# Infini-attention beside a gated MLP: gate logits on VectorE, finer buffers and pieces, and a new instruction order

## The chip, the cores and the metric

The kernel runs on one core of a Trainium2 chip. The metric is the device time of one execution in microseconds (us). A core has TensorE (PE, matmuls into PSUM), VectorE (DVE), ScalarE (ACT, activation functions), GpSimd (POOL) and SyncE (SP, which issues most DMAs). The engines run side by side; each one works through its own queue in order and waits there on semaphores.

## The reference, cut to what matters

A token's output is a mix of two branches, and the mixing weight comes from the token's gate logit `z = sum(x * gate_w)`:

```python
g = sigmoid((x * gate_w).sum(-1, keepdims=True))      # x: 2048 tokens x 512
return g * A(x) + (1 - g) * B(x)

def A(x):      # 32 heads of 16, 4 segments of 512 tokens
    q, k, v = x @ wq, x @ wk, x @ wv
    for s in range(4):
        p = softmax(q_s @ k_s.T * 0.25 + causal_mask)
        a_dot = p @ v_s
        a_mem = (phi(q_s) @ M) / (phi(q_s) @ z + 1e-6)
        o_s = sigmoid(beta) * a_mem + (1 - sigmoid(beta)) * a_dot
        M, z = M + phi(k_s).T @ v_s, z + phi(k_s).sum()
    return concat(o) @ wo
    # phi(t) = t + 1 where t > 0, else exp(t)

def B(x):      # 1792 hidden columns
    return (gelu_tanh(x @ w_gate) * (x @ w_up)) @ w_down
```

## The kernel before

All work is cut into named tasks. A list written out in the source, `ORDER` (lines 32 to 135), says in which order they are emitted, and so in which order each engine meets its own. `@A`, `@D`, `@P` behind a name choose ScalarE, VectorE or GpSimd; letters behind `#` name the buffers that the task takes. `Sched.run` (line 168) only checks that dependencies come earlier in the list. A task's number is segment and chunk, or, for logit slots, 0 to 79.

Tasks on TensorE. `mm4` (line 350) does a 128-column product as four 32-column tiles that run side by side, a round; before the first logit slot it is one matmul on the whole array (line 354), later four (line 358).

- `warm`, `xt`, `fill`, `k0f`: the start. x of segment 0 is transposed on TensorE, copied to `xT` (`ext`, in two token halves), and `k0f<fc>.<half>` makes the first k.
- `q`, `k`, `v`, `up`: groups of four rounds of 512 columns into one of two PSUM banks `gen` (a, b). `eq`, `ek`, `ev`, `eup` empty them; `ko` makes the copy of k for odd heads.
- `gt<s>.<pair>`: a pair of gate groups into a two-bank tile `lg` (three of them, a to c); `egt` is its gelu on ScalarE.
- `lg<n>`: a slot of logits for part of eight heads, twenty slots a segment (five for each chunk c of eight heads), in row tiling, into two `lg` tiles. `ex<n>a`, `ex<n>b` are the exps on ScalarE (line 662) into one of twelve `pT` buffers, `as<n>a/b` the causal masks on GpSimd (line 671).
- `pv<s>.<c>e/o`: probabilities times v for even and odd heads; it needs the masks of three slots. `epv`, `r`, `rg`, `n`, `m`, `o` on VectorE (and `m` on GpSimd) normalize, add the memory part and transpose back into `xT`.
- `M`, `den`, `num`: memory update and readout; `rma`, `rmr`, `rmg`, `nm` scale it. `E`, `Q`, `Em`, `ph`: phi; `pk`: its transpose by DMA, issued on SP.
- `dn<s>.<qt>.<hs>` (14 rounds) and `wo<s>.<qt>.<c>` (4 rounds) add up an output tile of 128 tokens in one bank; `os` scales it into one of four `osb` buffers, `st` stores it.
- `gz` (line 506): the gate logits of all tokens as 16 matmuls with `gate_w` repeated in 32 columns (`gwB`); `egz` transposes them, `zsp` (32 small GpSimd copies, lines 523 and 524) spreads them into `G2` and `omz`, `g2` and `omz` make the mixing weights. `bps` spreads beta with a small matmul, `tb` is its tanh.

`G`, the gated hidden values, has one buffer of 14 x 512 columns per segment, three in turn. In slots 1 and 4 of a chunk the logits come in pieces of 2, 1 and 1 blocks of 128 columns (line 630), and `pv` reads them as 2, 1 and 1. The last output tile is one bank, read in two halves:

```python
halves = [(0, D // 2), (D // 2, D)] if split else [(0, D)]
...
for n, (lo, hi) in zip(("DVE", "ACT"), halves):
```

Of the kernel before, what the change touches and what calls it, by code (L numbers as in the profile page):

```python
# [8 lines left out]
AF = mybir.ActivationFunctionType  # L9
# [23 lines left out]
in.x3 in.x2 in.x1 in.wo in.wup in.be in.gw in.wga in.wv in.wg0 in.wq in.wk in.wka in.xb in.xn  # L33
warm#a warm.free open#babca xt0.0 xt1.0 xt2.0 xt3.0 fill ext0.0 ext1.0 ext2.0 k0f0.0 k0f1.0 xt0.1
xt1.1 xt2.1 ext0.1 xt3.1 ext1.1 ext2.1 ext3.0 k0f0.1 ext3.1 k0f1.1 k0f2.0 k0f3.0 k0f2.1 k0f3.1
q0.2#a ek0.0@A ek0.1@D q0.3#b ko0.0@P Ek0.0 gt0.0#b eq0.3@D eq0.2@D ek0.3@A Qk0.0 gt0.1#c ek0.2@D
egt0.0 Emk0.0 ko0.1@D phk0.0 q0.0#b v0.2#a egt0.1 gt0.5#a Ek0.1 gt0.3#b egt0.5 gt1.4#c eq0.0@A
gt1.0#a ev0.2@A egt0.3 gt1.2#b egt1.0 egt1.4 gt0.4#a egt1.2 gt1.5#c egt0.4 pk0.0 gt0.6#b gt1.1#a
egt0.6 wdn egt1.5 gt1.3#b egt1.1 gt0.2#c egt1.3 bps#b gt1.6#a egt0.2 ebps v0.0#a egt1.6 lg0#bc
ev0.0@D v0.1#b ex0a#a q0.1#a ev0.1@D omg v0.3#b eq0.1@D ex0b#b as0a lg1#ab ev0.3@D up0.0#a ex1a#c  # L40
as0b up0.1#b eup0.0 ex1b#d Emk0.1 lg2#ca eup0.1 up0.2#a ex2a#e as1b gwB up0.3#b eup0.2 ex2b#f
Qk0.1 lg3#bc eup0.3 up0.4#a ex3a#g as2b as2a up0.5#b eup0.4 ex3b#h as1a lg4#ab eup0.5 up0.6#a
ex4a#i up0.7#b eup0.6 ex4b#j as4a lg5#ca eup0.7 pv0.0e#a as4b ex5a#k ko0.2@D up0.8#b phk0.1
epv0.0e ex5b#l lg6#bc eup0.8 up0.9#a ex6a#a up0.10#b eup0.9 as3b pk0.1 ex6b#b as3a lg7#ab ko0.3@P
eup0.10 pv0.0o#a ex7a#c up0.11#b epv0.0o ex7b#d as6b lg8#ca eup0.11 up0.12#a as6a ex8a#e as7b
up0.13#b eup0.12 as5b ex8b#f as7a lg9#bc eup0.13 gz#a as8a ex9a#g as8b as5a up1.0#b egz ex9b#h
as9a lg10#ab zsp eup1.0 pv0.1e#a ex10a#i up1.2#b epv0.1e ex10b#j lg11#ca eup1.2 up1.1#a ex11a#a
k1.0#b eup1.1 ex11b#b lg12#bc ek1.0@D k1.1#a ex12a#k r0.0 q1.0#b ek1.1@A as9b g2 up1.3#a eq1.0@A
as11b ex12b#l pv0.1o#b eup1.3 lg13#ab Ek1.0 rg0.0 epv0.1o as12b up1.4#a as12a ex13a#c up1.5#b
as10a eup1.4 as11a ex13b#d lg14#ca eup1.5 as10b up1.6#a Emk1.0 ex14a#e n0.0 q1.1#b eup1.6 ex14b#f  # L50
# [12 lines left out]
lg25#ab eup2.3 as20b q2.1#b ex25a#i o0.2 pv1.0e#a nm1.1@D eq2.1@A as25a lg26#ca epv1.0e ex25b#j
num1.2#b as24b enum1.2 up2.4#a as24a ex26a#a nm1.2@P dn0.0.0#b eup2.4 dn0.0.1 ex26b#b dn0.0.2
lg27#bc o0.1 as25b dn0.0.3 dn0.0.4 as26a ex27a#k rg0.3 num1.3#a dn0.0.5 as26b dn0.0.6 enum1.3
dn0.0.7 dn0.0.8 ex27b#l as27a lg28#ab n0.3 pv1.0o#a Ek2.0 as27b dn0.0.9 epv1.0o dn0.0.10 dn0.0.11
dn0.0.12 ex28a#c Emk2.0 dn0.0.13 wo0.0.0 o0.3 pv1.1e#a ex28b#d Qk2.0 as28a wo0.0.1 lg29#ca epv1.1e
wo0.0.2 ex29a#e ko1.2@D wo0.0.3 as28b up2.5#a os0.0@D ex29b#f ko1.3@D lg30#bc st0.0 r1.0 up2.6#b
pk1.1 eup2.5 ex30a#g as29b v2.0#a eup2.6 as29a ex30b#h rg1.0 lg31#ab ev2.0@D pv1.1o#b ex31a#a
dn0.1.0#a epv1.1o dn0.1.1 dn0.1.2 dn0.1.3 ex31b#b n1.0 lg32#ca phk2.0 dn0.1.4 v2.2#b ex32a#i  # L70
dn0.1.5 ev2.2@D dn0.1.6 ex32b#j lg33#bc dn0.1.7 v2.3#b as31a ex33a#c as32b dn0.1.8 ev2.3@D dn0.1.9
ex33b#d as30b lg34#ab as32a dn0.1.10 dn0.1.11 ex34a#e as31b dn0.1.12 dn0.1.13 wo0.1.0 m1.0@P
up2.7#b ex34b#f lg35#ca as34a eup2.7 wo0.1.1 ex35a#k wo0.1.2 as34b wo0.1.3 up2.8#b as33b os0.1@A
as30a lg36#bc as33a eup2.8 v2.1#a r1.1 nm1.3@D k2.2#b ev2.1@A Eq2.0 dn0.2.0#a ek2.2@D dn0.2.1
# [976 lines left out]
```

## Time and profile before

| | |
|---|---|
| time, median of 3 runs | 275.52 us (275.51 to 275.94) |
| profiled execution: span, first to last instruction | 274.6 us (274.58); its own time is not given apart |
| mean granted TensorE clock | 0.997 |
| TensorE / ScalarE / VectorE / GpSimd busy | 97 / 81 / 59 / 57% |
| ScalarE table loads | 13, 1.283 us each |
| exps | 160, 153.9 us busy |
| HBM read / written | 8.13 / 2.10 MB |
| SP's x2 and x3 transposes | issued from 16.86 to 29.0 us |
| `wup` issued, landed | 14.36 us, 8.5 us later |

A busy PE includes time in which matmuls are pipelined, so a share of 97% doesn't say that no time is lost; the distance from one start to the next does. Tables are loaded on ScalarE when it changes between exp and gelu.

### The profile page before, as it was taken

The page shows a single profiled execution, that of the slowest core. Times are in us where ns is not written, and L with a number is a line of the kernel's source. Part 1 is how long each engine was busy: PE and PEld are TensorE (multiplying, and loading weights), DVE is VectorE, ACT ScalarE, POOL GpSimd, SP SyncE. Part 2 cuts the span into 40 slices and gives each one's busy share as a digit, 9 for nine tenths or more (in the row PEclk, how much of TensorE's full clock was granted, in tenths as well). Part 3 has the DMA queues.
Part 4 walks back from the last instruction along what each step waited for, and adds up shares of the span by engine and source line. Part 5 has one row for each costly group of instructions (what it writes and reads, how often), then busy time and mean ns, then how long its engine had stood idle before and what let it go on. Part 6 is the DMA issues. An engine that isn't in the chain of part 4 may idle for free.

```text
span 274.6 us, 10880 instructions
## 1 busy us (share of the span) xinstructions
PE 267.1 (97%) x4877; PEld 132.2 (48%) x4877; DVE 162.7 (59%) x309; ACT 222.6 (81%) x242; POOL 156.5 (57%) x285
## 2 busy tenths in 40 slices
PE   8999999999999999999999999999999999899994
PEld 7644444444445554444455564444454454354551
DVE  1420017765889568887366757767558768376361
ACT  2598569989999968999877888989999997869411
POOL 8230003798634966864915847675467667887600
PEclk9999999999999999999999999999999999999998
DMA  7998780020002000002004200000000001001002
GB/s 228 363 252 191 165 258 2 2 42 4 4 2 41 5 2 0 2 5 60 2 2 80 43 24 0 2 2 21 2 5 21 2 2 41 21 5 41 21 5 78
DMA packets 22231, 14.07 MB, mean 51 GB/s; under 512 B 14120, under 2 KB 21160, under 8 KB 22184
## 3 DMA queue, kind: packets, MB, share of 16 engines
q1 hardware_dynamic: 21208, 12.52, 17.9%
q8 instruction: 38, 0.62, 1.0%
q10 hardware_dynamic: 976, 0.85, 0.9%
q14 instruction: 9, 0.07, 0.1%
HBM read 8.13 MB, written 2.10 MB: 37 GB/s over the span
## 4 chain that ended last, share of the span: by engine, by line
PE 86%; DVE 5%; POOL 4%; DMA 2%; issue 1%; ACT 0%; SPq 0%; POOLq 0%; DVEq 0%
PE dn L358 20%; PE up L358 17%; PE gt L354 9%; PE lg L639 8%; PE gt L358 8%; PE pv L690 6%; PE v L358 4%; PE k L358 4%; PE q L358 4%; POOL rm L869 3%; PE k L354 2%; DMA wk<-in_A_wk_dram 1%; DVE G L562 1%; PE q L354 1%; DMA out_dram<-osb 1%
## 5 line engine op out<-in xcount | busy, mean ns | idle before, releaser
L662 ACT ACTIVATE pT<-lg 128x1024 bf16<-128x1024 f32 x160 | 153.9, 1025 | 14.0 <-PE lg L639 11.4
L671 POOL TENSOR_SCALAR_AFFINE_SELECT pT<-pT 128x512 bf16<-128x512 bf16 (+1 forms) x160 | 86.7, 571 | 63.9 <-ACT pT L662 63.5
L358 PE MATMUL dn<-wdn,G 128*32 128x512 bf16 x896 | 61.4, 380 | 0.9 <-DVE Tm L896 0.9
L358 PE MATMUL up<-xT,wup 128*32 128x512 bf16 x896 | 56.3, 380 | 0.4 <-DVE T L708 0.2
L562 DVE TENSOR_TENSOR G<-up,G 128x512 bf16<-128x512 f32 x56 | 38.5, 688 | 26.4 <-PE up L358 25.0
L553 ACT ACTIVATE G<-gt 128x1024 bf16<-128x1024 f32 x28 | 27.8, 1023 | 11.6 <-PE gt L354 6.4
L358 PEld LDWEIGHTS <-wup 128*32 128x32 bf16 x896 | 23.1, 96 | 22.8 <-issue 4.5
L358 PEld LDWEIGHTS <-G 128*32 128x32 bf16 x896 | 22.7, 96 | 20.6 <-issue 4.1
L708 DVE STREAM_TRANSPOSE T<-pv 128x512 f32<-128x512 f32 x32 | 22.8, 713 | 14.2 <-PE pv L690 13.9
L216 DVE CAST vz<-v 128x512 bf16<-128x512 f32 x13 | 9.0, 689 | 30.2 <-PE v L354 24.2
L358 PE MATMUL gt<-xT,wga 128*32 128x512 bf16 x448 | 26.4, 379 | 0.0
L354 PE MATMUL gt<-xT,wga 128*128 128x512 bf16 x112 | 24.7, 379 | 0.0
L690 PE MATMUL pv<-pT,vz 128*32 128x256 bf16 (+2 forms) x640 | 23.4, 273 | 0.2 <-DVE osb L968 0.2
L690 PEld LDWEIGHTS <-vz 128*32 128x32 bf16 x640 | 15.3, 97 | 9.9 <-issue 1.3
L358 PE MATMUL dn<-wo,xT 128*32 128x512 bf16 x256 | 19.7, 380 | 0.0
L765 POOL TENSOR_TENSOR pkT<-E,Q 128x1024 bf16<-128x1024 bf16 x6 | 12.9, 2148 | 11.3 <-DMA pk<-pkT 5.6
L358 PEld LDWEIGHTS <-wga 128*32 128x32 bf16 x448 | 13.4, 97 | 10.1
L869 POOL TENSOR_SCALAR rm<-Tm 32x32 f32<-32x32 f32 x48 | 13.7, 286 | 7.2 <-DVE Tm L863 4.2
L639 PE MATMUL lg<-qT,kT 16*128 16x256 bf16 (+2 forms) x320 | 17.4, 274 | 0.0
L639 PE MATMUL lg<-qT,kO 32*128 32x128 bf16 (+2 forms) x320 | 17.2, 272 | 0.2 <-POOL kO L387 0.2
L358 PEld LDWEIGHTS <-xT 128*32 128x32 bf16 x480 | 11.7, 96 | 11.2 <-issue 2.2
L354 PEld LDWEIGHTS <-wga 128*128 128x128 bf16 x112 | 10.9, 98 | 13.0
(98 smaller groups left out, 297.7 us busy)
## 6 DMA issues: line engine op xcount, KB each, us to landing
out_dram<-osb SPq DMA_DIRECT2D x15, 128.0 KB, 1.7
wup<-in_B_w_up_dram SPq DMA_DIRECT2D x1, 1792.0 KB, 8.5
wdn<-in_B_w_down_dram SPq DMA_DIRECT2D x1, 1792.0 KB, 8.3
wga<-in_B_w_gate_dram SPq DMA_DIRECT2D x1, 1280.0 KB, 8.8
wga<-in_B_w_gate_dram SPq DMA_DIRECT2D x1, 512.0 KB, 6.2
wv<-in_A_wv_dram SPq DMA_DIRECT2D x1, 512.0 KB
wo<-in_A_wo_dram SPq DMA_DIRECT2D x1, 512.0 KB, 4.7
wdn<-in_A_x_dram ACTq DMA_DIRECT2D x1, 256.0 KB, 4.5
```

Source lines behind the costliest of these rows:

```text
L216: nc.vector.tensor_copy(dst, src)
L354: nc.tensor.matmul(out, lhsT=lhsT, rhs=rhs, start=start, stop=stop)
L358: nc.tensor.matmul(out[a], lhsT=lhsT[:, a], rhs=rhs, start=start, stop=stop, tile_position=(0, 32 * j), skip_group_check=True)
L553: nc.scalar.activation(G[s][:, 2 * hp:2 * hp + 2, :], t[:, :, :], AF.Gelu_apprx_tanh)
L562: UPT[(s, hs)] = evac("DVE", g, box, lambda e, t: nc.vector.tensor_mul(G[s][:, hs, :], t[:, :], G[s][:, hs, :]), kind="up")
L639: nc.tensor.matmul(A[j // 2][:, j % 2, at * P:(at + nq) * P], lhsT=l, rhs=r, start=True, stop=True, tile_position=(32 * j, 0))
L662: nc.scalar.activation(pT[(s, t, h)][:, :, :], A[h][:, :, :], AF.Exp, scale=0.25)
L671: nc.gpsimd.affine_select(out=v, in_=v, pattern=pat, compare_op=ALU.is_ge, fill=0.0, base=0, channel_multiplier=-1)
L690: nc.tensor.matmul(t[32 * j:32 * j + 32, qb * P:(qb + nq) * P], lhsT=vz[s % 2][:, kt, h * VW:h * VW + 32], rhs=pT[(s, t0 + w, j // 2)][:, ...
L708: nc.vector.transpose(TT[key][:, e, :, :].rearrange("p a b -> p (a b)"), t[:, :])
L765: nc.gpsimd.tensor_add(d[:, :, :], box["E"][:, :, :], box["Q"][:, :, :])
L869: eng_of[e].tensor_scalar_add(RMt[s][32 * j:32 * j + 32, c, :, :], bx["Td"][32 * c:32 * c + 32, :, 2 * j:2 * j + 2], 1e-6)
```

## The change

- The gate logits are sums on VectorE: x is loaded a second time in rows (segments 1 to 3 into unused parts of the `wdn` and `wo` buffers), and sixteen `z<s>.<kt>` multiply a 128 x 512 block by `gate_w` and sum along the row. `gz`, `egz`, `gwB` go. `wdn` is loaded once all z are done, `wo` once those of segment 3 are.
- beta is loaded already spread, in eight small DMAs; `bps` goes.
- Pieces of slots 1 and 4 are 3 blocks and 1 block. Their masks become two instructions of 128 x 256.
- `G` is 21 buffers of one pair each.
- The first k does both early feature chunks, then the other two, for the first token half before the second half.
- The last tile's two column halves are two accumulations in two banks, each with 14 + 4 rounds of 256 columns.
- All rings have their buffers named in the list, some dependencies that only kept an order are dropped, and `ORDER` is new.

```diff
@@ loads
-    nc.sync.dma_start(gw[:, :], gate_w.rearrange("(fc p) -> p fc", p=P))
-    nc.sync.dma_start(beta8[:, :], A_beta.rearrange("(c h) -> h c", h=8))
+    nc.sync.dma_start(gwb, gate_w[None, :].to_broadcast((P, D)))
+    for s in range(1, NSEG):
+        nc.sync.dma_start(xr[s], x2[s * L:(s + 1) * L, :].rearrange("(kt p) d -> p kt d", p=P))
+    for h in range(8):
+        nc.sync.dma_start(beta[DH * h:DH * h + DH, :],
+                          A_beta.rearrange("(c h) -> h c", h=8)[h:h + 1, :].to_broadcast((DH, NCH)))
     for s in range(2, NSEG):
         load_x(s)
-    load_w(nc.sync, wo, A_wo)
@@ first_k
-        for f in range(2):
-            for h in range(2):
+        for h in range(2):
+            for f in range(2):
@@ gate_rows
+        def f_z(s, kt):
+            nc.vector.scalar_tensor_tensor(out=xr[s][:, kt, :], in0=xr[s][:, kt, :], scalar=1.0,
+                                           in1=gwb, op0=ALU.mult, op1=ALU.mult,
+                                           accum_out=zc[:, s, kt:kt + 1])
...
         def f_sp(e):
+            for a in range(4):
                 for j in range(4):
                     nc.gpsimd.tensor_copy(
+                        G2[32 * j:32 * j + 32, :, :].rearrange("p s (k a) -> p a s k", a=4)[:, a],
+                        zc[32 * a:32 * a + 32, :, :])
...
+        TAB["wdn"] = add("wdn", "SP", lambda _: load_w(nc.sync, wdn, B_w_down), kind="wdn",
+                         deps=zs)
+        TAB["wo"] = add("wo", "SP", lambda _: load_w(nc.sync, wo, A_wo), kind="wol",
+                        deps=zs[3 * KT:])
@@ logit_slot
-            parts = [(e1, 1, 1, 2, 0), (e1, 1, 3, 1, 3), (e1, 3, 3, 1, 2)]
+            parts = [(e1, 1, 1, 3, 0), (e1, 3, 3, 1, 3)]
...
+                    vs = [pt[:, :, 0:P], pt[:, :, 3 * P:]][:1 if w in (0, 3) else 2]
@@ pv_group
-            for w, kt, qb, nq, at in ((w0, 0, 0, 4, 0), (w0 + 1, 1, 1, 2, 0),
-                                      (w0 + 1, 1, 3, 1, 3), (2, 2, 2, 2, 2 * e),
-                                      (w0 + 1, 3, 3, 1, 2)):
+            for w, kt, qb, nq, at in ((w0, 0, 0, 4, 0), (w0 + 1, 1, 1, 3, 0),
+                                      (2, 2, 2, 2, 2 * e), (w0 + 1, 3, 3, 1, 3)):
@@ out_group, the last tile
+        for n, (lo, hi) in enumerate([(0, D // 2), (D // 2, D)]):
+            g, first, fe = out_part(s, qt, f"{s}.{qt}h{n}", lo, hi, ring, "dn", late, bx)
```

The new list, in three passages (start, middle of segment 3, end). In it the first logit slot stands before most gate pairs of segment 0, and gate pairs are spread among the slots.

```
... ext0.1 xt3.1 ext1.1 ext2.1 ext3.0 ext3.1 k0f2.0 k0f3.0 k0f0.1 k0f1.1 k0f2.1 k0f3.1
ek0.0@A ko0.0@D#a q0.2#aa gt0.1#b q0.0#bb ... gt0.0#c ... gt0.3#a egt0.3#c q0.3#a lg0#bc v0.0#b ex0b#a
ex0a#b gt1.4#a egt1.4#d ... up0.3#a eup0.3 z0.1 ... v0.2#a lg1#cb z3.0 ev0.2@D ev0.3@A up0.4#b up1.0#a ...
...
... lg71#cb pv3.1o#b ... rma3@P#a ex71b#l ... lg75#ca ... as74b as71a as75b ... rmr3 mbd2 os2.1@D#b pv3.2e#aa rmg3
...
... dn3.2.13 wo3.2.0 wo3.2.1 wo3.1.2 wo3.2.2 dn3.0.10 wo3.2.3 os3.2@A#b wo3.3h0.1 dn3.0.11
wo3.1.3 dn3.0.12 wo3.3h0.2 dn3.0.13 wo3.0.0 dn3.3h1.0#a os3.1@A#c st3.1 st3.2 dn3.3h1.1 wo3.0.1
wo3.0.2 wo3.0.3 os3.0@D#d st3.0 st2.3 wo3.3h0.3 os3.3h0@A#c st3.3h0 dn3.3h1.2 dn3.3h1.3 ...
wo3.3h1.0 wo3.3h1.1 wo3.3h1.2 wo3.3h1.3 os3.3h1@A st3.3h1
```

More of the change, by code (lines that the diff above doesn't have):

```diff
@@ L32 @@
 ORDER = """
[L33 to L50, printed above, removed]
@@ new lines @@
+in.xb in.xn warm#a warm.free open#babcaab xt0.0 xt1.0 xt2.0 xt3.0 fill ext0.0 ext1.0 ext2.0 k0f0.0
+k0f1.0 xt0.1 xt1.1 xt2.1 ext0.1 xt3.1 ext1.1 ext2.1 ext3.0 ext3.1 k0f2.0 k0f3.0 k0f0.1 k0f1.1
+k0f2.1 k0f3.1 ek0.0@A ko0.0@D#a q0.2#aa gt0.1#b q0.0#bb ek0.2@A ek0.1@D ek0.3@D Ek0.1#a Qk0.1#a
+ko0.1@P gt0.0#c eq0.2@A egt0.1#a egt0.0#b eq0.0@A gt0.3#a egt0.3#c q0.3#a lg0#bc v0.0#b ex0b#a
+ex0a#b gt1.4#a egt1.4#d ev0.0@D eq0.3@A gt1.2#c gt0.2#b q0.1#b up0.3#a eup0.3 z0.1 ko0.2@D#b
+egt1.2#e egt0.2#f eq0.1@A gt1.0#a egt1.0#g v0.3#b v0.2#a lg1#cb z3.0 ev0.2@D ev0.3@A up0.4#b
@@ L597 @@
     gate_rows()
-    g, box = group("", "bps", 60, f_bps, [a_be])
-    t_tb = evac("ACT", g, box, lambda e, t: nc.scalar.activation(
-        tb[:, :], t[:, 0:NCH], AF.Tanh, scale=0.5), kind="tb")
+    t_tb = add("tb", "ACT", lambda e: nc.scalar.activation(
+        tb[:, :], beta[:, :], AF.Tanh, scale=0.5), kind="tb", deps=[a_be])
     t_om = add("omg", "DVE", f_omg, kind="omg", deps=[t_tb])
     t_eb = add("eb", "DVE", f_eb, kind="eb", deps=[t_om])
-    t_wo = add("wos", "DVE", f_wo, kind="wos", deps=[t_om, a_wo])
-    def order(gi, h):
-        s, t = divmod(gi, NSLOT)
-        return [GM[(min(s + 1, NSEG - 1), hp)] for hp in range(HS // 2)] if t + h == 0 else []
+    t_wo = add("wos", "DVE", f_wo, kind="wos", deps=[t_om, TAB["wo"]])
     LT, XT_, AT, NMT, OTT = {}, {}, {}, {}, {}
@@ L921, in store, with out_part @@
         eng.dma_start(out2[q0:q0 + P, lo:hi], osb[:, lo:hi])
[L923 to L925 removed]
+    def out_part(s, qt, tag, lo, hi, ring, name, late, bx):
         box = {}
[L927 to L938 removed]
@@ L963, in fn, with fe @@
+        for c in range(NCH):
+            def fn(_, c=c):
+                mm4(box["t"][:, 0:hi - lo], xT[:, c, s * L + qt * P:s * L + (qt + 1) * P],
+                    wo[:, c, lo:hi], False, c == NCH - 1)
+            prev = add(f"wo{tag}.{c}", "PE", fn, cost=MM * (hi - lo) // D,
+                       deps=[prev, t_wo, OTT[(s, c)]])
+        def fe(e):
+            if "o" not in bx:
                 bx["o"] = rtile("osb", [P, D])
@@ L965, in fn, with out_group @@
             if e == "ACT":
[L966 removed]
+                nc.scalar.activation(bx["o"][:, lo:hi], box["t"][:, 0:hi - lo], AF.Copy, scale=g)
             else:
[L968 to L971 removed]
+                nc.vector.tensor_scalar_mul(bx["o"][:, lo:hi], box["t"][:, 0:hi - lo], g)
+        return prev, first, fe
+    def out_group(s, qt):
+        end = s == NSEG - 1
+        ring = "lg" if end and qt > 0 else "gen"
+        late = [LT[NSEG * NSLOT - 1]] if ring == "lg" else []
+        bx = {}
+        if (s, qt) != (NSEG - 1, KT - 1):
+            g, first, fe = out_part(s, qt, f"{s}.{qt}", 0, D, ring, "dn", late, bx)
+            ev = add(f"os{s}.{qt}", ["DVE", "ACT"], fe, kind="os", deps=[g, TAB["omz"]],
+                     alloc=["osb"], frees=[(ring, first)])
             add(f"st{s}.{qt}", "SP", lambda _: store(nc.sync, s, qt, bx["o"], 0, D), kind="st",
```

353 lines of the change are left out of this document (151 added, 202 removed).

## The prediction

> **What bounds the kernel now.** I read the page's first part, then the timeline of TensorE, then the chain of waits, then the start, the end and ScalarE's timeline.
>
> ```profile
> PE 267.1 (97%) x4877; PEld 132.2 (48%) x4877; DVE 162.7 (59%) x309; ACT 222.6 (81%) x242; POOL 156.5 (57%) x285
> ```
>
> TensorE (PE) is the bound; ScalarE is second. PE's timeline (start, length) shows what each piece costs, by start to next start:
>
> ```profile
> 46.73 0.40 PE L639 MATMUL lg<-qT,kO 32*128 32x512 bf16 x4
> 47.05 1.91 PE L358 MATMUL up<-xT,wup 128*32 128x512 bf16 x32
> 48.89 0.40 PE L639 MATMUL lg<-qT,kO 32*128 32x256 bf16 x12
> 49.22 1.91 PE L358 MATMUL up<-xT,wup 128*32 128x512 bf16 x32
> 51.07 0.40 PE L639 MATMUL lg<-qT,kT 16*128 16x512 bf16 x4
> ...
> 55.42 0.73 PE L690 MATMUL pv<-pT,vz 128*32 128x512 bf16 x20
> 55.98 1.04 PE L358 MATMUL up<-xT,wup 128*32 128x512 bf16 x16
> ...
> 59.44 1.05 PE L506 MATMUL gz<-xT,gwB 128*32 128x512 bf16 x16
> 60.32 1.04 PE L358 MATMUL up<-xT,wup 128*32 128x512 bf16 x16
> ```
>
> A logit slot with two `up` groups lasts 2.16 to 2.18 us, so with 0.865 for a group (four rounds of 512 columns at 0.216) a slot costs 0.44, its slower successor included. `pv` takes 0.55, a gate pair 1.73, `M` 0.24. From the end of the first k (10.44) to PE's end (270.73) the order then holds: q, k, v, up 100 x 0.865 = 86.5; gt 28 x 1.73 = 48.44; dn, wo, num, den 303 x 0.216 = 65.45; pv 17.6; lg 80 x 0.44 = 35.2; M 1.44; gz 0.865; bps 0.17: 255.66 us. The stretch is 260.29 long, so only 4.63 us are waits. Window by window, from one `lg` to the next, the sum fits to 0.03 us except in a few: lg22, 24, 26, 41, 43, 45 are 0.31 to 0.41 too long (2.10 together), lg72 and 73 1.58, seven others 0.07 to 0.15 (0.78), the rest 0.17. The chain names the six:
>
> ```profile
> 170.21 0.70 DVE G L562
> 170.95 1.05 PE k L358 x16
> ...
> 175.16 0.70 DVE G L562
> 175.90 1.05 PE k L358 x16
> ```
>
> There are two `gen` banks. Where a bank's next user follows after only `lg` and `num` (0.44 + 0.22 = 0.66 us of PE work), VectorE hasn't emptied it: from the stall this needs about 1.0. The two long ones hang on GpSimd's `rma3`, sixteen instructions at L869 which VectorE waits for:
>
> ```profile
> 239.97 0.40 PE L358 MATMUL dn<-wdn,G 128*32 128x512 bf16 x4 [0.92 <-DVE Tm L896]
> ```
>
> The end: PE stops at 268.83 + 1.90 = 270.73, but ScalarE waited for an `osb` buffer, then VectorE for ScalarE on the same bank, and 3.85 us pass to the span's end at 274.58.
>
> ```profile
> 268.83 1.90 PE L358 MATMUL dn<-wo,xT 128*32 128x512 bf16 x32
> 270.14 1.17 ACT L966 ACTIVATE osb<-dn,omz 128x512 bf16<-128x512 f32 x2 [2.55 <-DMA out_dram<-osb]
> 271.34 0.48 DVE L968 TENSOR_SCALAR osb<-dn,omz 128x256 bf16<-128x256 f32 x1 [3.26 <-ACT osb L966]
> ```
>
> **The change, part by part.** Each on PE's path unless said.
>
> *Gate logits.* `gz` (0.865) and `bps` (0.17) leave PE: -1.04. `gwB`, `egz` and half of `zsp` leave VectorE and GpSimd, off the path. VectorE gets 16 products with a sum, 128x512 bf16. No row shows this form; the nearest are 0.40 (L731, bf16) and 0.90 (L585), so 6.4 to 14.4 us; I take 0.6, the spacing of VectorE's other 512-column products (L562): 10 us. They stand beside lg0 to lg9, where VectorE's work, these included, is 26 us against 45 of PE. Cover gone, each would delay an emptied bank by its length.
>
> *Loads.* SP issues the gate row, three 512 KB row blocks (0.5 us each, like `gw`) and eight small beta loads (0.62 each, the row of `beta`) ahead of the x2 and x3 transposes, so these end near 35 instead of 29; their first user is k2.0 behind lg11, after 60. `wup` landed at 14.36 + 8.5 = 22.9. The 1.7 MB behind it, at the 294 to 345 GB/s of 16 to 24 us, are in by 28 to 29; z3.0, the first that needs them, comes behind lg1, near 30. `wdn` and `wo` are queued on SP behind the z's; only later transposes and stores stand behind them. wdn's first user is dn0.0.0, behind lg24. Cost 0, margin of the rows about 2 us.
>
> *384-column pieces.* 32 sets of four matmuls fewer in `lg` and 32 in `pv`, the same columns. The quoted rows price them: 12 matmuls in a slot or 4, both 0.32 to 0.33 to the next start; `pv` at 0.55 is ten 128-column blocks of 0.054, with nothing over. I take 0; ends -0.3 (10 ns in each of 32 slots) and 0. GpSimd pays: in 64 halves one 0.655 select becomes two of 0.446, +15 us, and seven more `ko` at 1.56, +11; with less `zsp` about 179 us (65%), off the path while a `pv` finds its masks done.
> [...]
>
> *First k by halves.* Now PE waits from 7.29 for the first copies of the second half:
>
> ```profile
> 6.84 0.61 PE L448 MATMUL xt<-wdn 128*128 128x128 bf16 x8
> 7.80 0.94 ACT L214 ACTIVATE xT<-xt 128x256 bf16<-128x256 f32 x3 [2.90 <-DVE xT L216]
> 7.82 2.78 PE L354 MATMUL k<-xT,wk 128*128 128x256 bf16 x24 [0.36 <-DVE xT L216]
> ```
>
> k0f2.0 can fill 7.29 to 7.72. But k0f3.0 needs ext3.0, which stays behind ext1.1 on ScalarE: second of three in 0.94, done at 8.43. So k0f3.0 starts near 8.46 and five pieces of 0.435 end at 10.65: +0.21. Were ext3.0 not late, -0.53; those are the ends.
>
> *G in pair buffers* (21 x 2 KB for 3 x 14 KB): no instruction changes, 0.
>
> *Last tile in two banks.* 36 rounds of 256 columns at 0.108 for 18 of 0.216: PE 0. Its first half is emptied while PE works on the second. After PE's end 0.03 + 0.48 (one 256-column copy) + 2.76 (from 271.82 to 274.58 now) = 3.27 for 3.85: -0.58. Cover: os3.3h0 waits for st3.1 in buffer c; os3.1 can start 0.14 after wo3.1.3 (behind os3.2), takes 0.68, its store 2.04 (chain of waits), then 0.48: 3.4 against 3.46 of PE work. Without that cover, up to 0.5.
>
> *New order.* Counting PE work between users of a `gen` bank in the two lists: before, six times 0.66 and twelve times 0.86 to 0.87; after, none under 0.98. The missing time to 1.0 sums to 4.3 before and 0.5 after. rma3 now starts behind lg71 and its first reader, nm3.0, stands behind lg79. I drop 2.10 + 1.58 + 0.17 of waits, keep the 0.78, add 0.52: 1.30 left.
> Price: ScalarE switches between exp and gelu 21 times instead of 13, +10.3 us:
>
> ```profile
> 98.75 2.97 ACT L553 ACTIVATE G<-gt 128x1024 bf16<-128x1024 f32 x3 [2.76 <-PE gt L358]
> 101.74 1.28 ACT L662 ACT_TABLE_LOAD   x1
> 103.03 1.94 ACT L662 ACTIVATE pT<-lg 128x1024 bf16<-128x1024 f32 x2
> ```
>
> From a gate pair's end, gelu and load need 0.2 (PE's end of a group to its reader's start) + 0.92 (1.94 - 1.02, one of two back to back) + 1.28 = 2.4. The new list puts 1.41 to 1.95 of PE work between that end and the next `lg`, whose exps could start 0.53 later: ScalarE is late by 0 to 0.46, and the next slot, 1.54 to 2.17 on, needs only the first exp (1.45 to 1.9). Cost 0 to 0.4, in the 0.78.
> [...]
>
> **Sum.** 10.65 + 254.62 + 1.30 + 3.27 = 269.84 us of span. The profiled span, 274.58, lies 0.94 under the median 275.52; with that added, **270.8**. Break-even is 6.0 us of waits in place of 1.30.
>
> **Rivals.**
> 1. GpSimd late (slower). With 22 us more, in clumps, a mask comes after its `pv` wants it. Place: pv3.2e behind lg75, where rma3 (5.5) and eight masks stand ahead and the margin is 0.3; pv1.1e behind lg30 has 0.5. For: selects last up to 1.09. Against: GpSimd itself waits 63.5 us at L671 now, all for exps not there yet. 0.3 us at each of the 32 `pv` = 9.6: 279.1. It decides from 0.15 each. 8%.
> 2. Loads on the path (slower). Without lead, each window after a switch lacks load and exps minus its PE work, 10.3 us: 279.8. It decides from 4.7 of the 10.3. 5%. [...]
> 3. Late rows: z3.0 blocks VectorE's queue, with ev0.2 and eup1.0 behind it, and PE runs out of banks. 3 us late over the margin: 273.8; break-even at 4.7. 10%.
> 4. The spacing doesn't hold on the chip because VectorE, busier, serves banks late: as many waits as now, 4.63: 274.1. 13%.
> 5. Pieces pay after all: `M`, eight sets of 34 columns (0.0143 each) in 0.24, holds 0.016 a set beyond its columns; on 64 sets 1.0: 269.8. 2%.
> The forecast has 62%, with its own range 269.0 to 272.6 (waits 0 to 3, first k and the ends above).
>
> **How the numbers follow.** The range 269.0 to 275.0 takes in the forecast, 3 (part), 4 and 5, and leaves out most of 1 and 2 and late ends of 3. 0.2% (0.55 us) is about what a measurement can tell. Faster: 62 + 2 + 12 of case 4 + 8 of case 3 = 84%; same 3% (1 each of 1, 3, 4); slower 7 + 5 + 1 of case 3 = 13%.
>
> **What would show it.** Right: PE's stretch from first k to its end near 256 us; no `k` or `up` behind `DVE G L562` in the chain; 21 loads, yet PE's windows behind them at their sums; the last copy to span's end 2.8; the first k ending near 10.65, with PE idle near 7.7. Wrong: `pv` behind `POOL pT L671`, `up` behind a z or a DMA in 25 to 40 us, or `lg` behind ACT at lg1, 5, 18, 21, 25, 52.

## The result, and the profile after

The changed kernel takes 287.2 us (median of 283.72, 285.83, 289.50, 288.58) against 275.73 for the kernel before (275.51 to 276.45). The ratio is 1.0326 (95%: 1.0281 to 1.0371), made from the two quicker of those four executions, as the others are over 1.5% above the quickest. The kernel is slower by 3.3%; 270.8 was predicted, faster. The profiled execution took 283.72, with a span of 282.0: 12.9 us above the forecast, which can be followed below. The other 3.5 us up to the median lie in executions that have no profile.

The page's first part, to be held against the row of before (in later rows: start and length in us, engine, line, operation, tiles, shapes, count, and in brackets the idle time before and what ended it; SPq is SP issuing transfers):

```profile
PE 268.2 (95%) x4964; PEld 129.7 (46%) x4964; DVE 181.6 (64%) x328; ACT 232.1 (82%) x251; POOL 181.8 (64%) x338
```

TensorE is still the bound: it has as much to do as before and stands more. The work terms hold. In an undisturbed slot, lg6 to lg7, the next start is 2.17 us on, as before, though the slot has 8 matmuls and not 12. In TensorE's timeline of this execution the first k ends (the next group starts) at 10.60, behind the gap that was predicted:

```profile
8.42 2.35 PE L359 MATMUL k<-xT,wk 128*128 128x256 bf16 x20 [0.62 <-ACT xT L220]
```

So 277.94 (TensorE's end) - 10.60 - 254.62 (the sum of its work) = 12.7 us are waits, where the sum had 1.30. I call **slip** of a window what passes from one `lg` to the next beyond the work between them, at the prediction's prices. The slips of after sum to 12.2 us, and 10.8 of them lie in twelve windows: lg5 1.36; lg11, 12 0.95, 0.91; lg14 2.02; lg19, 22, 42, 51 0.91, 0.69, 0.69, 0.91; lg29, 39, 40 0.43, 0.53, 0.69; lg75 0.66. The profile shows what each waited for; that this is the cause is shown where a run below takes it away.

*lg5.* SP's queue. The eight small beta loads hold SP for 8.71 us (1.09 each), the transposes of x2 and x3 behind them end at 40.58, and pk0.1, behind those, is issued at 40.70:

```profile
17.67 2.02 SPq L305 DMA_DIRECT2D wo<-in_A_x_dram  x1
19.74 8.71 SPq L307 DMA_DIRECT2D beta<-in_A_beta_dram  x8
28.49 12.09 SPq L274 DMA_TRANSPOSE xT<-in_A_x_dram  x8
40.70 8.59 SPq L776 DMA_TRANSPOSE pk<-pkT  x4
```

On GpSimd phik0.0 waits for the `pkT` buffer that pk0.1 reads, and the masks wait behind phik0.0:

```profile
44.62 2.13 POOL L747 TENSOR_TENSOR pkT<-E,Q 128x1024 bf16<-128x1024 bf16 x1 [2.12 <-DMA pk<-pkT]
46.70 3.25 POOL L654 TENSOR_SCALAR_AFFINE_SELECT pT<-pT 128x256 bf16<-128x256 bf16 x7
```

```profile
49.28 0.72 PE L672 MATMUL pv<-pT,vz 128*32 128x512 bf16 x14 [0.98 <-POOL pT L654]
```

*lg19, 22, 42, 51 and part of lg11.* ScalarE's timeline: after the last gelu it waits for `lg`, and only then comes the table load. TensorE, two slots on, waits for the first exp:

```profile
90.80 1.02 ACT L551 ACTIVATE G<-gt 128x1024 bf16<-128x1024 f32 x1 [0.70 <-PE gt L363]
92.58 1.28 ACT L643 ACT_TABLE_LOAD   x1 [0.75 <-PE lg L622]
93.87 1.94 ACT L643 ACTIVATE pT<-lg 128x1024 bf16<-128x1024 f32 x2
```

```profile
94.26 0.33 PE L622 MATMUL lg<-qT,kO 32*128 32x384 bf16 x2
94.95 0.39 PE L622 MATMUL lg<-qT,kO 32*128 32x384 bf16 x6 [0.36 <-ACT pT L643]
```

*lg11, 12.* ScalarE's g2 waits for the 16 copies of `zsp` on GpSimd, ahead of exps:

```profile
68.53 0.26 ACT L528 ACTIVATE G<-G 128x64 f32<-128x64 f32 x1 [0.89 <-POOL G L523]
```

*lg14, 29, 39, 40.* VectorE stands still beside GpSimd. Four instructions that took 0.74 us before (first line) now take 3.35; the next fence is GpSimd's at the same time. One by one they take 0.31, 0.44, 0.67 and 2.17 us, and each ends 0.05 us after a GpSimd instruction does: the first three after a mask, the fourth after the addition.

```profile
78.41 0.74 DVE L581 TENSOR_SCALAR bdeb<-bd,ebr 128x128 bf16<-128x128 bf16 x4
72.89 3.35 DVE L570 TENSOR_SCALAR bdeb<-bd,ebr 128x128 bf16<-128x128 bf16 x4
```

```profile
74.07 2.12 POOL L747 TENSOR_TENSOR pq<-E,Q 128x1024 bf16<-128x1024 bf16 x1
```

TensorE then waits for a bank that VectorE empties behind them:

```profile
76.89 1.05 PE L363 MATMUL up<-xT,wup 128*32 128x512 bf16 x16 [1.51 <-DVE G L559]
```

*The end.* From TensorE's last matmul (277.94) to the span's end are 4.1 us, 3.27 predicted. SP issues six stores, and is done with the last one 1.3 us after its copy ended (279.70 against 278.44). One of the six took 1.28 us to issue, the others 0.33 to 0.49:

```profile
275.24 4.46 SPq L893 DMA_DIRECT2D out_dram<-osb  x6
277.06 0.47 ACT L922 ACTIVATE osb<-dn,omz 128x256 bf16<-128x256 f32 x1 [1.85 <-DMA out_dram<-osb]
277.97 0.47 ACT L922 ACTIVATE osb<-dn,omz 128x256 bf16<-128x256 f32 x1 [0.43 <-PE dn L363]
```

### The profile page after: what moved, and what is told of

It reads as the page before. It is cut to its first block, busy times and chain, and to the rows that moved or that the text cites. A ratio compares the mean times of both kernels' runs of the same rounds, so it can differ in the third digit from the quotient of the medians.

```text
span 282.0 us, 11156 instructions
## 1 busy us (share of the span) xinstructions
PE 268.2 (95%) x4964; PEld 129.7 (46%) x4964; DVE 181.6 (64%) x328; ACT 232.1 (82%) x251; POOL 181.8 (64%) x338
## 4 chain that ended last, share of the span: by engine, by line
PE 50%; POOL 13%; DVE 10%; SPq 9%; DMA 6%; issue 5%; ACT 4%; ACTq 0%; POOLq 0%; DVEq 0%
PE dn L363 14%; PE up L363 10%; SPq L274 7%; PE gt L363 7%; POOL pT L654 7%; PE lg L622 5%; PE pv L672 4%; POOL rm L851 4%; DMA wo<-in_A_x_dram 4%; ACT pT L643 4%; PE q L363 3%; PE k L363 3%; PE v L363 3%; DVE N L708 2%; DVE G L559 2%
## 5 line engine op out<-in xcount | busy, mean ns | idle before, releaser
L654 POOL TENSOR_SCALAR_AFFINE_SELECT pT<-pT 128x256 bf16<-128x256 bf16 (+1 forms) x224 | 101.2, 489 | 48.9 <-ACT pT L643 48.4
L363 PE MATMUL dn<-wdn,G 128*32 128x512 bf16 (+1 forms) x952 | 59.0, 368 | 0.0
L363 PE MATMUL gt<-xT,wga 128*32 128x512 bf16 x800 | 46.0, 379 | 0.0
L363 PEld LDWEIGHTS <-wga 128*32 128x32 bf16 x800 | 22.1, 97 | 19.7 <-issue 0.2
L672 PE MATMUL pv<-pT,vz 128*32 128x384 bf16 (+3 forms) x512 | 23.6, 300 | 1.2 <-POOL pT L654 1.0
L622 PE MATMUL lg<-qT,kT 16*128 16x512 bf16 (+3 forms) x256 | 18.6, 302 | 2.1 <-ACT pT L643 2.1
L392 POOL TENSOR_SCALAR kO<-kT,odd 128x512 bf16<-128x512 bf16 x10 | 16.0, 1598 | 5.7 <-DVE kT L222 5.6
L363 PE MATMUL dn<-wo,xT 128*32 128x512 bf16 (+1 forms) x272 | 18.9, 367 | 0.0
L622 PE MATMUL lg<-qT,kO 32*128 32x256 bf16 (+3 forms) x256 | 17.9, 300 | 0.4 <-ACT pT L643 0.4
L363 PE MATMUL v<-wv,xT 128*32 128x512 bf16 x256 | 16.3, 380 | 0.8 <-ACT osb L922 0.8
```

The costliest lines, as they stand in the source:

```text
L363: nc.tensor.matmul(out[a], lhsT=lhsT[:, a], rhs=rhs, start=start, stop=stop, tile_position=(0, 32 * j), skip_group_check=True)
L392: eng_of[e].tensor_scalar_mul(QK[ko][:, c % 2, :], QK[("k", s, pr)][:, c % 2, :], odd[:, :])
L622: nc.tensor.matmul(A[j // 2][:, j % 2, at * P:(at + nq) * P], lhsT=l, rhs=r, start=True, stop=True, tile_position=(32 * j, 0))
L654: nc.gpsimd.affine_select(out=v, in_=v, pattern=pat, compare_op=ALU.is_ge, fill=0.0, base=0, channel_multiplier=-1)
L672: nc.tensor.matmul(t[32 * j:32 * j + 32, qb * P:(qb + nq) * P], lhsT=vz[s % 2][:, kt, h * VW:h * VW + 32], rhs=pT[(s, t0 + w, j // 2)][:, ...
```

## The experiments

All start from the changed kernel. Code of an edit is shown once; words of `ORDER` are moved or added as said.

| run | median us | profiled span | sum of slips | ratio to before, 95% |
|---|---|---|---|---|
| a1_preload | 280.90 (three) | - | - | 1.0198 (1.0154 to 1.0242) |
| a2_beta | 282.40 | 281.7 | 13.7 | 1.0234 (1.0187 to 1.0281) |
| a3_eb | 287.20 | 287.1 | 16.3 | 1.0385 (1.0342 to 1.0429) |
| a4_pieces | 288.28 | 285.4 | 17.5 | 1.0445 (1.0419 to 1.0472) |
| b1_start | 282.46 | 280.3 | 10.9 | 1.0231 (1.0203 to 1.0259) |
| b2_start_pre | 282.07 | 280.9 | 9.8 | 1.0211 (1.0179 to 1.0243) |
| b3_four | 279.55 | 278.1 | 8.1 | 1.0121 (1.0089 to 1.0153) |
| b4_phi | 279.60 | 278.0 | 8.5 | 1.0125 (1.0101 to 1.0149) |
| c1_best | 275.30 | 274.0 | 4.6 | 0.9992 (0.998 to 1.0004) |
| c2_best_pieces | 277.18 | 274.3 | 5.9 | 1.006 (1.0037 to 1.0082) |
| c3_wait / c4_wait_fill | 283.36 / 280.46 | 281.6 / 278.8 | 11.5 / 9.7 | one execution each |
| d1_best2 | 274.83 | 272.3 | 3.9 | 0.9961 (0.9944 to 0.9978) |
| d2_best2_nopre | 277.77 | 275.4 | 6.9 | 1.0064 (1.0042 to 1.0087) |
| d3_best2_store | 274.36 | 272.6 | 3.9 | 0.9937 (0.9919 to 0.9956) |

### One cause at a time

**a1_preload.** `px0` to `px10` in `ORDER`, each behind the last gelu or tanh ahead of exps:

```diff
+    pre = ctile("pre", [P, 1], F32)
...
+        if word[:2] in ("px", "pg") and word[2:].isdigit():
+            fun = AF.Exp if word[1] == "x" else AF.Gelu_apprx_tanh
+            add(word, "ACT", lambda e, fun=fun: nc.scalar.activation(
+                pre[:, :], odd[:, :], fun), kind="pre")
```

> The changed kernel with eleven one-column Exp activations added on ScalarE, one right behind the last gelu (or tanh) ahead of each return to exp, so that the exp tables are loaded while TensorE still works on the group before the next lg; the value of the tiny activations is used nowhere. Theory (a table load is issued only after the wait of the activation that needs it, and the first exp waits for lg): the five places where a load stood behind ScalarE waiting for lg (65.3, 92.6, 104.5, 169.5, 191.9 us, idle 0.75 to 1.5 before the load) lose that wait; the slips at lg11, 19, 22, 42, 51 (0.6 to 0.9 each) go, the profiled span falls from 282.0 by 3.0 to 4.1 us. Rival (ScalarE is late by its sum anyway, the load only moves the waiting): the loads move but the span falls by less than 1.2. Rival (the added 11 instructions of about 0.2 us put ScalarE later): no change or slower by up to 2.

Its profiled execution took 1482.8 us, with TensorE shown busy throughout, for a reason that isn't known, and isn't used; the other three took 280.53 to 282.74. Two of the three spans, 278.6 and 278.7, lie where the theory had them, the third at 281.0; without a profile the windows can't be read, and b2 and d2 settle it.

**a2_beta.**

```diff
-    for h in range(8):
-        nc.sync.dma_start(beta[DH * h:DH * h + DH, :], ...
+    a_be = add("ldb", "SP", load_beta, kind="ldb")    # ORDER: pk0.1#a ldb
```

> The changed kernel with the eight small beta loads issued on SP behind pk0.1 instead of ahead of the x2 and x3 transposes. Theory (SP spends about 1.09 us on each of the eight, so the transposes and pk0.1 behind them start 8.7 us late, phk0.0 on GpSimd waits for the pkT buffer until 44.6, the masks follow, pv0.0e waits): the transposes end near 32 instead of 40.6, pk0.1 is issued when phk0.1 is ready (near 37 to 39), GpSimd's wait of 2.1 at 42.5 shrinks below 0.5 and the slip of lg5 (1.36) falls below 0.4; span -1.0 to -1.4. Rival (the masks of lg5 are late because GpSimd has too much, not because of its wait): the wait goes but lg5 still slips by over 0.8.

lg5's slip went from 1.36 to 0, as the theory said, and the same eight loads took SP 3.86 us (0.48 each) behind the transposes. But the transposes now ran beside the last row block, which came late: z3.0 held VectorE, and lg1 and lg2 slipped by 2.68 and 0.76. (The transposes took 15.95 us for 12.09, so they ended at 36.2, not near 32.)

```profile
30.95 0.69 DVE L513 SCALAR_TENSOR_TENSOR wo<-wo,wdn 128x512 bf16<-128x512 bf16 x1 [3.39 <-DMA wo<-in_A_x_dram]
```

This is the prediction's rival 3, which the slow beta loads had been covering up.

**a3_eb.** In `ORDER`: `eup1.3 eb ko1.0@P`.

> The changed kernel with eb (six VectorE instructions that make bdeb) moved from behind epv0.1o to behind eup1.3, some 5 us earlier, away from GpSimd's phq1.0. Theory (VectorE's bf16 instructions stand still while GpSimd runs an add of two bf16 tiles; bdeb took 3.35 us beside phq1.0 of 2.12): bdeb falls to about 0.7 to 1.0, eup0.7 starts about 2 us earlier, lg14's slip of 2.02 falls below 0.5; span -1.4 to -1.9. Rival (the four bdeb instructions are slow in themselves or by their wait on omg): they keep over 2.5 us at the new place. Rival (lg14 hangs on something else): slip stays over 1.2.

bdeb fell from 3.35 to 0.74 us and lg14's slip from 2.02 to 0.72: shown. Yet the run was slower, since lg5 and lg6 slipped by 4.79 and 1.91. The edit comes later than they do and can't have caused it; pk0.1 was issued at 43.63 this time, not 40.70, and its first half landed 4.2 us after its issue, not 2.7; phik0.0 waited 5.43 us, and TensorE stood for 3.88. What came next, in stretches of 1 us (length; busy time and instructions of PE, PEld, DVE, ACT, POOL; then granted clock, DMA share, GB/s):

```profile
51.00:52.00 1.00, 0.00 (x0) 0.00 (x0) 0.00 (x0) 0.00 (x0) 1.00 (x4) 1.00 0.10 20
52.00:53.00 1.00, 0.28 (x4) 0.13 (x7) 0.00 (x0) 0.00 (x0) 1.00 (x4) 0.51 0.57 111
55.00:56.00 1.00, 1.00 (x16) 0.33 (x12) 0.31 (x2) 1.00 (x2) 0.00 (x0) 0.50 0.00 0
```

From 52.0, still in the standstill, until near 58.8 TensorE's granted clock is 0.50 (0.79 over 58 to 60), and the two q groups behind the standstill take 3.60 us for the 1.91 of after; that makes lg6's slip and a part of lg5's.

**a4_pieces.**

```diff
-            parts = [(e1, 1, 1, 3, 0), (e1, 3, 3, 1, 3)]
+            parts = [(e1, 1, 1, 2, 0), (e1, 1, 3, 1, 3), (e1, 3, 3, 1, 2)]
... (pv and the masks as before)
```

> The changed kernel with the 384-column pieces undone: three pieces 2+1+1 in lg and five in pv as before, and one mask instruction for a half instead of two. Theory (the pieces gain nothing on TensorE and cost GpSimd 64 instructions): TensorE's windows keep their sums (a slot with two ups 2.17, pv 0.55), GpSimd's busy time falls by 12 to 17 us from 181.8, and of the waits only those that hang on late masks shrink (lg5 1.36, lg75 0.66): span -0.5 to -1.8. Rival (the pieces paid): TensorE's undisturbed windows grow by 0.016 a set, together +1.0. Rival (GpSimd's load is what makes VectorE late everywhere): span -3 or more.

Inconclusive: lg5 and lg6 slipped by 4.65 and 1.74 here too (3.75 us of standstill, two q groups in 3.44 us for 1.91, a mean clock of 0.987). Here the queue is not to blame: pk0.1 was issued at 40.98, almost as in after, but its second half landed 4.4 us after its issue, not 2.5; why isn't known. Undisturbed slots stayed at 2.17. Repeated on a steadier start as c2.

### The start, and a ladder of repairs

**b1_start.** a2 with `z0.3 z3.0` in place of `lg1 z3.0`.

> The changed kernel with its start mended: the eight beta loads on SP behind pk0.1 (as in a2_beta) and z3.0 moved on VectorE from behind lg1 to behind z0.3 (past lg2), so that VectorE doesn't stand 3.4 us for the last row block. Theory (the large and changing part of the loss is the start: rows, betas, transposes and pk0.1 on one SP queue; with TensorE idle for 1.7 us or more its clock is then granted at 0.5 for some 3 to 6 us, which doubles the loss): lg1, lg2, lg5, lg6 lose their slips, no slice shows a lower clock, the profiled span is 282.0 - 1.4 = 280.6 within 0.6, and the four times agree within 1 us instead of 6. Rival (the slip goes to the next window that needs the same data, lg7 to lg9 by way of z's or pk0.0): sum of slips over 12. Rival (the spread comes from elsewhere): times still spread by 3 us or more.

lg1 and lg5 slip no more, the span is 280.3, and the four times lie within 1.05 us (282.03 to 283.08), where those of after spread over 5.8. So the start most likely makes both the spread and, in the worse executions, the largest single loss. The other three executions of after have a mean clock of 0.987 to 0.993, like a3's 0.988; that they stood at lg5 as a3 did is likely, but they have no profile.

**b2_start_pre.** b1 and a1 together.

> b1_start with the eleven one-column Exp activations of a1_preload. Theory (a load stands behind the first exp's wait on lg in five places): lg11, 19, 22, 42, 51 fall from 4.2 us of slips together to below 1.0; span 3 to 4 us below b1_start. Rival (ScalarE is late by its sum): less than 1.2 below.

lg19, 22, 42, 51 fell from 3.2 to 0.4, but the span did not: px1 with its load stood ahead of a copy (ev0.3) that TensorE waits for, which cost 1.14 in lg1, and 0.68 came back in lg43 and lg44. That leaves 1.1 gained in the slips; this execution lost it outside them, with a wait of 1.29 for gate weights ahead of lg0 and an end 0.75 longer. The placing was wrong, not the mechanism (d2). lg11 stayed at 0.96: it has two causes, and either one alone keeps it there (here g2, in d2 the load).

**b3_four.** b2 with `eb` as in a3 and `g2` behind `ex12b`.

> b2_start_pre with eb behind eup1.3 (as in a3_eb, which took lg14 from 2.02 to 0.72) and with g2 on ScalarE moved behind ex12b, so that it doesn't wait for zsp ahead of ex10b, ex11, ex12. Theory: lg14 falls by 1.3, what is left of lg11 and lg12 (about 1.2 together) goes; span 2.0 to 2.6 us below b2_start_pre, some 275 us in time or less. Rival (the eb part only moves TensorE's wait to lg15 or lg16, and g2 later makes rg0.1 and n0.1 late on VectorE): below b2_start_pre by under 1.0.

2.5 us gained in time, 1.7 of it in the slips; lg12 lost all its slip, lg11 0.69 of 0.96. But lg15 now slips 1.70: bdeb, moved away, takes 0.74, and the next VectorE instruction with both inputs in SBUF stands still in its place, beside the same GpSimd add (0.65 to 1.07 elsewhere, except 1.81 beside another such add, in lg29):

```profile
74.16 2.66 DVE L717 TENSOR_TENSOR N<-T,r 128x512 bf16<-128x512 f32 x1
```

```profile
74.15 2.13 POOL L756 TENSOR_TENSOR pq<-E,Q 128x1024 bf16<-128x1024 bf16 x1
```

**b4_phi.** The two instructions of each phi become one on VectorE, and the words `Em` go:

```diff
-            nc.vector.tensor_scalar_min(box["E"][:, :, :], box["E"][:, :, :], 1.0)
...
-            nc.gpsimd.tensor_add(d[:, :, :], box["E"][:, :, :], box["Q"][:, :, :])
+            nc.vector.scalar_tensor_tensor(out=d[:, :, :], in0=box["E"][:, :, :], scalar=1.0,
+                                           in1=box["Q"][:, :, :], op0=ALU.min, op1=ALU.add)
```

> b3_four with each phi (min of the exp with 1, then plus relu) made by one VectorE instruction in place of a VectorE min and a GpSimd add of two 128x1024 bf16 tiles (14 adds of 2.1 us leave GpSimd); phk0.0 stands behind eq1.1. Theory (VectorE's two-input and fast bf16 instructions stand still beside GpSimd's two-tile adds): what is left at lg29, 39, 40, 44, 58, 63, 64 (2.5 us together in the changed kernel) shrinks below 1.2, no VectorE zbd, N or Mbd takes over 1.2 us; span 1 to 2 us below b3_four; GpSimd about 30 us less busy. Rival (the fused instruction costs VectorE 1.2 us where the min cost 0.4, in front of the copies that TensorE waits for): same as b3_four or slower by up to 2.

lg15, lg39 and lg40 improved (1.70 and 0.54 to under 0.1, 0.70 to 0.10), which shows GpSimd's additions as their cause. lg29 did not (0.38), so its cause stays open. And lg16, 23, 37, 61, 68 slipped by 4.4 together where the fused form, mostly 1.2 to 1.4 us, stands ahead of a bank's emptying. No change in sum: it pays only where VectorE has the room.

**c1_best.** b3 with px1 behind ev0.3, the fused form for three phis only (at the place of their min), and `st2.3` behind `st2.0`.

> b3_four with: the second early Exp (px1) behind ev0.3 instead of ahead of it; phiq1.0, q2.0 and q2.1 made by one VectorE instruction each at the place of their min (no GpSimd add); the store st2.3 issued behind st2.0 instead of behind st3.0. Theory (each remaining loss has its own cause): lg1's 1.14 goes (the load stood ahead of a copy that TensorE waited for), lg15's 1.70, lg40's 0.70 and lg39's 0.54 shrink to 0.6 together (N, zbd and Nm stood still beside GpSimd's two-tile adds), the span ends 3.3 instead of 4.1 us behind TensorE's last matmul; span 278.1 - 1.1 - 2.3 - 0.8 = 273.9, time near 275.6, the same as the kernel before. Rival (VectorE, now 1.2 instead of 0.4 us for three phis, is late elsewhere): span above 276.

275.30 for 275.6 expected: the time of the kernel before (0.9992, with 1 in the interval). The fused q2.0 was ill placed (lg39 1.33), and the end had not shortened.

**c2_best_pieces.** a4's edit on c1.

> c1_best with the 384-column pieces undone (three pieces in lg and five in pv, one mask instruction for a half, as in a4_pieces, now with a start that doesn't vary). Theory (they gain nothing on TensorE): undisturbed windows keep their sums (2.17 with two ups), GpSimd is 10 to 15 us less busy, time within 0.6 us of c1_best. Rival (they pay 0.016 a set): +1.0 us, undisturbed windows longer by 0.06. Rival (their 64 extra GpSimd instructions hold VectorE or masks up): -1 or more.

Slower by 1.9 us. Undisturbed slots are 2.17 in both, so the pieces pay nothing on TensorE; the added slips are at lg9, 24, 53, 70. At lg24 VectorE's min took 0.81 instead of 0.38; beside it GpSimd has four masks in 2.91 us, three of them of 512 columns, where the new form has six in 3.38, five of them of 256. Shorter GpSimd instructions holding VectorE less would explain it; this was not tested by itself. The slips show 1.3 of the 1.9; the profiled spans differ by only 0.3, as c2's end is 1.0 shorter.

### The clock by itself

**c3_wait and c4_wait_fill.** c3 is c1 with as0b's mask made eleven times; c4 is c3 with matmuls ahead of pv0.0e:

```diff
-                for v in vs:
+                for v in vs * (11 if (s, t, h) == (0, 0, 1) else 1):
...
+            for _ in range(56 if (s, c, e) == (0, 0, 0) else 0):
+                mm4(t[:, 0:P], warm, warm, True, True)
```

> c1_best with the mask of as0b made eleven times over instead of once (the same select, same result), so that pv0.0e waits for GpSimd some 4 us longer. Theory (a TensorE that stood idle is granted half its clock for some us after): TensorE idle 3.5 to 4.5 us near 50, then a granted clock of 0.50 for 3 to 7 us; the span grows by the idle time and 1.5 to 3.5 us more, 6 to 7 in all. Rival (the low clock of the disturbed runs came from the disturbed transfers or from the chip): clock 1.00 throughout, span + 4.

> c3_wait with 224 matmuls of 128 columns, about 3.0 us of TensorE work on zeros into pv0.0e's own bank, issued ahead of pv0.0e, where TensorE would wait for the masks; pv0.0e itself overwrites them. Theory (idling lowers the clock): idle near 1 us, clock 1.00 throughout, span below c3_wait by 1.5 to 3.5 us though 3 us of matmuls are added. Rival: same as c3_wait or longer.

Stretches of c3, then of c4 (columns as above):

```profile
49.00:53.00 4.00, 0.34 (x6) 0.00 (x0) 0.87 (x3) 1.51 (x2) 3.46 (x9) 0.84 0.15 33
53.00:56.00 3.00, 2.25 (x30) 0.96 (x33) 0.96 (x2) 0.35 (x1) 1.35 (x4) 0.50 0.00 0
56.00:59.00 3.00, 3.00 (x40) 0.98 (x32) 1.10 (x4) 1.59 (x2) 1.34 (x4) 0.57 0.00 0
```

```profile
49.00:53.00 4.00, 2.96 (x212) 2.79 (x200) 0.64 (x1) 1.27 (x2) 3.44 (x9) 1.00 0.15 36
53.00:56.00 3.00, 2.86 (x57) 1.38 (x60) 1.71 (x4) 1.34 (x2) 1.13 (x3) 1.00 0.03 5
56.00:59.00 3.00, 3.00 (x56) 1.10 (x52) 1.35 (x3) 2.49 (x6) 1.84 (x5) 1.00 0.02 5
```

TensorE stood for 4.41 us in c3. lg5 and lg6 slip by 7.0 us together in c3 and by 4.8 in c4, with the same wait for GpSimd and 3 us of work more: the clock fell to 0.50 in c3's pause and stayed at 1.00 in c4, where TensorE stood for 1.18 us only. (The spans, 281.6 and 278.8, differ by 2.8, partly for other reasons: c4's end is 0.85 shorter, and its lg53 slips by 0.5.) Each is one execution.

### What is left

**d1_best2.** c1 with phiq2.0 behind eM1.0 and phik0.1 fused.

> c1_best with the fused phiq2.0 moved on VectorE from ahead of enum1.1 to behind eM1.0, and phik0.1 fused too. Theory (lg39's 1.33 in c1_best is M1.0 waiting for a transpose that stood behind the fused phi; lg4's 0.43 is ScalarE waiting for phik0.1 on GpSimd): both go, span 274.0 - 1.1 - 0.4 = 272.5, time near 274.1, faster than the kernel before by 0.3 to 0.6%. Rival (each repair only hands the wait on): as c1_best, 275.3.

0.9961 (0.9944 to 0.9978): faster than both kernels, by 0.4% against the one before (single times overlap: 273.96 to 276.24 against 275.34 to 276.72). lg39 fell to 0.19 and lg4 to under 0.1; 0.7 came back at lg43 and lg44. The page's first part:

```profile
PE 266.0 (98%) x4963; PEld 129.1 (47%) x4964; DVE 178.9 (66%) x328; ACT 232.7 (85%) x262; POOL 175.4 (64%) x334
```

**d2_best2_nopre.** d1 without `px0` to `px10`.

> d1_best2 without the eleven early Exp activations. Theory (a load behind the first exp's wait costs TensorE 0.6 to 0.9 in each of lg11, 19, 22, 42, 51): these slips come back, time 2.5 to 3.5 us above d1_best2. Rival (ScalarE late by its sum): less than 1.0 above.

2.94 us slower; lg11, 19, 22, 42, 51 sum to 4.15 against 0.6. In d1 the load follows the gelu at once, and the exp finds its table there:

```profile
85.39 1.02 ACT L554 ACTIVATE G<-gt 128x1024 bf16<-128x1024 f32 x1 [0.70 <-PE gt L366]
86.44 1.28 ACT L596 ACT_TABLE_LOAD   x1
87.73 0.20 ACT L596 ACTIVATE pre<-odd 128x1 f32<-128x1 f32 x1
87.84 1.92 ACT L652 ACTIVATE pT<-lg 128x1024 bf16<-128x1024 f32 x2
```

**d3_best2_store.** Two of the last stores by `nc.gpsimd` instead of `nc.sync`.

> d1_best2 with the stores of tiles 3.0 and 3.2 issued by GpSimd instead of SP. Theory (the end is SP issuing five stores of 0.9 us each one behind the other, the last one issued 1.4 us after its copy): the last store is issued by its copy's end, the span ends 0.7 to 1.0 us earlier behind TensorE's last matmul. Rival (the end is the landing of the last store, whoever issues the others): no change; or GpSimd's issue is slower and the end later.

The rival: spans 272.6 and 272.3, the last copy to the span's end 3.0 and 2.8 us. The theory had misread SP: each of d1's five issues at the end takes 0.33 us; the 0.9 was c1's mean, with waits for copies and one issue of 1.39 in it. The time, 274.36, lies within d1's 273.96 to 276.24.

## Why the prediction was wrong

Three terms that were put at nothing or nearly nothing failed. In the profiled execution the table loads hold up to 4.15 us of slips, VectorE stopped by GpSimd 3.2, zsp ahead of g2 0.9 in lg12 and a share of lg11, and SP's queue 1.36.

- *Work terms: right.* Gate logits off TensorE, no gain from the pieces in TensorE's slots, GpSimd 181.8 for 179, 21 loads, most of them followed at 0.01 by their activation. A z took 0.61 us from start to start when alone, as taken (0.6), and up to 1.09 beside GpSimd's masks. The first k's end, 10.60 for 10.65, is in part luck: over the profiled runs, with the same start of `ORDER`, it lies between 9.55 and 11.03, and the 0.62 gap is missing in five of them.
- *New order, "1.30 left": half right.* The bank shortages are gone: TensorE's `up` waits for `DVE G` in two places (1.8 us), both in lg14's window, where VectorE stands. What failed is taking all else as covered: 12.2 of slips for 1.30.
- *Loads, "Cost 0": the first step that failed.* Beta was priced at 0.62 each from a load issued on an emptier queue; it took 1.09. And the list of what stands behind on SP named the transposes, whose users are late, but not pk0.1, whose buffer GpSimd waits for. Price: 1.36 us in the profiled execution, up to 6.7 in a3's, where a slower landing and a clock of 0.50 were added. Rival 3 had the right cause (data behind a queue), with 10% and on another path; a2 shows its own path too.
- *Price of the loads, "0 to 0.4": the second.* The sum let the load start with the gelu's end. Where the exp had to wait for `lg`, it started only when `lg` was done, so the 1.41 to 1.95 of lead was worth nothing there: d2 against d1 gives 2.9 us. This is rival 2 at a third of its price.
- *GpSimd "off the path while a pv finds its masks done": the third.* GpSimd was late as rival 1 had it in one place only (lg75, 0.66, the place named; 0 in a2, which has the same order there). It cost more by stopping VectorE: lg14, 39, 40 sum to 3.2, with a3 as proof for lg14 and b4 for lg39 and lg40; lg29's 0.43 is open. zsp ahead of g2 (lg11, 12) was counted as "less `zsp`", and its wait not at all.
- *Last tile, -0.58: right in size, but not steady.* It was 4.1 us for 3.27 in after, where one store took 1.28 us to issue. In a2, with the same six stores (row below), none took over 0.50, and the end was 3.2. In a3 and b2 the last two stores took 3.4 and 3.6 us to land (1.6 in a2), and the end was 4.9 and 5.1; in d1 it was 3.3. Why issue and landing are sometimes slow isn't shown.

```profile
275.83 3.58 SPq L896 DMA_DIRECT2D out_dram<-osb  x6
```

- *0.94 added to the span: wrong by 0.8.* Time minus span is 1.7 in after's profiled execution; the 0.94 compared one execution's span with a median of others.

With the side effects taken out (d1), the sum's parts come back: 10.05 (end of the first k) + 254.62 + 3.85 + 3.34 = 271.9, span 272.3. Its median time, 274.8, is 4 us above the forecast. The profiled execution, 273.97, is 3.2 above: 2.6 of waits, 0.8 by which time exceeds the span beyond 0.94, 0.4 that the sum leaves over, less 0.6 for the first k.

## What to carry to other kernels

Of whatever is put ahead in a DMA queue, list all that stands behind it, down to the small transfer whose buffer an engine off the path waits for. Ahead of a return to another activation function, put a one-column activation of the new one at once behind the last of the old ones (not ahead of a copy that something waits for); it gained 2.9 us here. When VectorE is to do more, look at what GpSimd does at that moment, not at either one's share of busy time. Where TensorE must wait for some us, spare matmuls that fit into the wait can keep its clock up (1.00 in c4 for 0.50 in c3, and 2.2 us less in lg5 and lg6, from one execution each).

## What the runs showed of the hardware that was not expected

- TensorE's granted clock fell to 0.50 in pauses of 3.88 us (a3) and 4.41 us (c3), 3.2 and 2.4 us after their start, and stayed there for 6.8 us in both. In a2 it was 0.50 for 3.4 us from 32.4 on, right behind a pause of 1.68 us (rows below). In pauses of 1.51 us (after, clock 1.00 from 72 to 80) and 1.64 us (b3, where the `up` group behind it took 1.05, as elsewhere) it did not fall. What decides it stays open:

```profile
31.00:32.00 1.00, 0.00 (x0) 0.00 (x0) 1.00 (x3) 1.00 (x2) 0.00 (x0) 1.00 1.33 261
33.00:34.00 1.00, 1.00 (x12) 0.20 (x4) 0.00 (x0) 0.00 (x0) 0.00 (x0) 0.50 0.57 18
```

- While GpSimd added two 128x1024 bf16 tiles (2.1 us), some VectorE instructions ended only behind the addition. Two of them have two tiles in SBUF as inputs: N took 2.66 for 0.65 to 1.07 and ended 0.54 after it (b3), zbd 2.15 for 0.2 and 0.08 after it (after). So did bdeb, bf16 with one tile and one scalar column (2.17 in after for 0.25 before, 0.05 after it). `G<-up`, which reads one of its inputs from PSUM, kept its 0.68 to 0.69. What sets them apart isn't shown.
- In after, an exp's table load stood behind the exp's wait on `lg` in all five places where the exp had to wait (0.75 to 1.48 us); a gelu's load at 198.51 ran ahead of its 0.60 wait on `gt`. Why they differ stays open, as does why SP's small loads cost 1.09 us ahead of the transposes (after) and 0.48 behind them (a2).
